# Linear attention and a token/channel mixer on one core: the last 64 rows of k and v on all 128 partitions, their product in quarters of the array, and two first attention tiles moved next to a last one

## The chip, the cores and the metric

The kernel runs on 1 core of one Trainium2 chip. The metric is the device time of one execution in microseconds. A core has five engines that run side by side and wait for each other by semaphores: TensorE (PE, matrix products, with its weight loads shown as PEld), VectorE (DVE), ScalarE (ACT), GpSimd (POOL) and SyncE (SP). All of them work on SBUF, a memory of 128 partitions. TensorE writes its sums to PSUM, 8 banks of 2 KB per partition, from which ACT and DVE copy them away. Transfers between HBM and SBUF are issued from a queue (here nearly all from SP's, the stores of the attention stage from POOL's) and are carried by 16 DMA engines.

## The reference

All arrays are float32; the batch is 8, 8 heads, 576 rows (seq), 64 columns per head.

```python
def _attn_ref(q, k, v, g_norm):
    kv = np.einsum('bhsd,bhse->bhde', k, v)
    out = np.einsum('bhsd,bhde->bhse', q, kv)
    rms = np.sqrt(np.mean(out * out, axis=-1, keepdims=True) + 1e-06)
    return (out / rms * g_norm).astype(np.float32)

def _moe_ref(x, w_tok1, w_tok2, w_ch1, w_ch2):
    xt = x.transpose(0, 2, 1)
    h = np.maximum(xt @ w_tok1, 0.0) @ w_tok2
    u = x + h.transpose(0, 2, 1)
    h2 = np.maximum(u @ w_ch1, 0.0) @ w_ch2
    return (u + h2).astype(np.float32)
```

The attention's output, laid out as (8, 576, 512), is x of the second part. w_tok1 is 576x256, w_tok2 256x576, w_ch1 512x1536, w_ch2 1536x512. The change concerns the first line alone, kv = k by v: for each batch and head a 64x64 matrix, summed over the 576 rows.

## The kernel before

**Stages.** Eight batches are worked in four pairs (numbered 0 to 3). For each pair come k by v (`kv`), attention (q by kv, `attend`), the normalisation, and token mixing (`tok1`, `tok2`). The channel mixing (w_ch1, w_ch2) of all batches follows from about 183 us to the end; it is a long run of full-array matmuls built on Strassen-like sums. While attention runs, the weights w_ch1 and w_ch2 are fetched and decoded from raw words on ACT and DVE (the "rounding" steps).

**Names.** `side` is 0 or 1, the batch within a pair. `half` is 0 or 1, the left or right 256 of the 512 columns (four heads). A pair has 9 tiles of 128 rows: groups c = 0 and 1 are side 0's four, c = 2 and 3 side 1's four, and c = 4 is one tile with the 64 remaining rows of both sides. J = 4, JJ = 5, HF = 64, LO = 512, DH = 256, D = 64.

**k and v in SBUF.** A side's k lies in `k_in[side]`, 128 partitions by 5 blocks (JJ) of 512 columns: four blocks with 512 rows, and block J with the last 64 rows on partitions 0 to 63. Partitions 64 to 127 of block J are filled with zeros once, for each side, by `zero_rows` (steps `zz0`, `zz1`, on POOL). `load` (steps `l0`, `l1`) issues, for k and then for v, one transfer of the 512 rows (`load_rows`) and two of 32 rows and 512 columns for the rest (`load_rem`). Six such loads are issued for pairs 1 to 3; pair 0 is loaded in another way and takes no part in the change except that its `zz` steps go.

**k by v.** `kv(side, half)` runs 20 matmuls: for two column groups i, five blocks j and two heads h, one matmul of 128 rows, 64 weights columns and 64 moving columns. Head h writes to PSUM partitions 64h to 64h + 63, so two matmuls use the two column halves of the array. Each (side, half) has its own bank, from a pool of two named "kv". `evict` (`e00`, `e01`, ...) copies a bank to `kvp[side]` on ACT.

**Attention.** `attend(c)` (step `a{c}`) runs 32 matmuls of 64x64 in the four quarters of the array: 64 rows (one head's part of kvp), 64 weights columns (half a tile of q). It takes two banks, from the pool "kv" for c = 0 and "o" otherwise. Steps `q`, `g`, `t` read these banks (square on ACT, times g on DVE, sum on DVE); `m`, `r`, `i` make the inverse root; `s`, `p`, `d` scale a tile on ACT, POOL or DVE. `a4` (`attend_rem`, tile name ps_r) is the tile of remaining rows, 16 matmuls of the same kind.

**Token mixing.** `h{side}{t}` (tok1) runs full-array matmuls (128x128 weights, 512 moving columns) over four tiles; `hr` adds the remaining rows, in two row halves. `u{i}` (tok2) makes tile i; `u8`, the tile of remaining rows, uses two column halves. Its result is added on DVE and stored by three transfers from POOL's queue.

**Order.** The order on every engine is the order of the strings that `play` reads: `start` (pair 0), `middle` (attention of pair 1 among the mixing of pair 0), two lists `steady` (pairs 2 and 3), then `last`. A leading "-" means a step of the pair before, a number means that many rounding steps. Each engine runs its part of this order strictly in turn. The first lines of `steady[0]` are:

```python
"kv00 kv01 e00 e01 -d40 f3", "-u8 -a3 -q30 -g31 -q31 -g30 -t30 -t31 -m3 -r3 -lq1",
"h00 -i3 -d31 -s30 l0 b00 1 1", "h01 f4 x01 1", "a0 q00 g01 q01 g00", "h10 t00 t01 b01 x10 1",
```

So side 0's k by v is followed by u8 and a3 of the pair before, then by h00 and h01; a0 stands between h01 and h10; `l0` loads the next pair's k and v for side 0; `f` steps fetch raw weights, `lq` and `lr` fetch q. Side 1's k by v (`kv10 kv11`) stands behind a1. In the trace all matmuls carry the helper's line 136, all transfers line 124 and ACT's copies line 133, so the tile names tell them apart: ps_kv is k by v, ps_o and ps_r attention, ps_h tok1, ps_u tok2.

## Time and profile before

| what | value |
|---|---|
| median of 3 runs | 770.01 us (770.0 to 770.4) |
| the profiled execution's own time | 769.76 us |
| its span, first to last instruction | 767.9 us |
| mean granted TensorE clock | 1.000 |
| ps_kv matmuls (all pairs) | 640 records, 20.9 us |
| ps_o matmuls in quarters | 768 records, 13.9 us |
| POOL memsets of k_in and v_in | 4, 0.52 us each |

A matmul of float32 leaves two records in the trace, so 640 records are 320 matmuls. Starts and durations are in microseconds from the start of the span. Matmuls overlap, so the time of a group is best read from its start to the next group's start; the recorded end of a group lies a little after that.

### The profile page before, as it was taken

Reading aid. Unit: us, or ns where it says so; the run is one execution under the profiler, and the core shown is the slowest. Engines: PE = TensorE matmul, PEld = TensorE weight load, DVE = VectorE, ACT = ScalarE, POOL = GpSimd, SP = SyncE. Lnnn points to the kernel's source line nnn. Section 1 sums busy time; section 2 is a strip of 40 time slices with the busy share of each in tenths; the row PEclk is TensorE's granted clock in tenths of the full one; section 3 lists DMA queues with packets and bytes.
Section 4 is the critical chain, followed back from the end, with each engine's and each line's share of the span. In section 5 each row is a group of like instructions: output and inputs, shape, how many; then the busy total and the mean of one; then the engine's idle time right before and its main releaser. Section 6 shows DMA issues by size and latency. Waiting matters only on the chain.

```text
span 767.9 us, 12737 instructions
## 1 busy us (share of the span) xinstructions
PE 761.9 (99%) x4694; PEld 615.4 (80%) x4694; DVE 644.9 (84%) x958; ACT 279.5 (36%) x563; POOL 112.8 (15%) x125
## 2 busy tenths in 40 slices
PE   9999999999999999999999999999999999999997
PEld 8655555446888888888888888888888888888887
DVE  4868886997757779899968989997898997798996
ACT  3656666773210332512234241123352223325221
POOL 1003030204410000002240002042000227000204
PEclk9999999999999999999999999999999999999999
DMA  9999997599699785589997578999659889755679
GB/s 356 379 366 382 353 376 281 178 326 340 244 290 318 291 284 167 172 271 217 221 230 251 154 226 213 261 185 265 195 154 295 159 227 211 199 150 158 156 188 120
DMA packets 137981, 188.28 MB, mean 245 GB/s; under 512 B 48704, under 2 KB 95808, under 8 KB 135872
## 3 DMA queue, kind: packets, MB, share of 16 engines
q1 hardware_dynamic: 102240, 168.72, 68.3%
q0 software_dynamic: 34848, 18.36, 15.9%
q8 instruction: 38, 0.62, 0.3%
q10 hardware_dynamic: 832, 0.39, 0.2%
q14 instruction: 23, 0.19, 0.1%
HBM read 138.28 MB, written 49.15 MB: 244 GB/s over the span
## 4 chain that ended last, share of the span: by engine, by line
PE 96%; DMA 2%; DVE 1%; SPq 0%; ACT 0%; issue 0%; DVEq 0%
PE ps_d L136 28%; PE ps_b L136 19%; PE ps_a L136 19%; PE ps_u L136 8%; PE ps_h L136 8%; PE ps_v L136 5%; PE ps_c L136 3%; PE ps_w L136 2%; PE ps_kv L136 2%; PE ps_o L136 2%; DMA raw<-in_moe_w_tok_dram 1%; DMA v_in<-in_k_dram 1%; PE ps_r L136 0%; DVE x L494 0%; DVE ms L522 0%; DVE w_tok L211 0%
## 5 line engine op out<-in xcount | busy, mean ns | idle before, releaser
L136 PE MATMUL ps_d<-ui,w 128*128 128x256 f32 x504 | 118.6, 379 | 0.0
L136 PEld LDWEIGHTS ps_d<-ui,w 128*128 128x128 f32 x504 | 96.0, 190 | 12.8
L133 ACT COPY ps_d<-ps_a 128x768 f32<-128x768 f32 (+1 forms) x56 | 32.0, 572 | 199.9 <-PE ps_a L136 196.9
L127 DVE TENSOR_TENSOR v<-v,v 128x1536 f32<-128x1536 f32 (+2 forms) x70 | 103.3, 1483 | 0.3
L136 PE MATMUL ps_b<-sv,w 128*128 128x256 f32 x324 | 78.9, 380 | 0.0
L136 PE MATMUL ps_a<-v,w 128*128 128x256 f32 x324 | 78.8, 379 | 0.0
L1275 POOL DMA_DIRECT2D out_dram<-us x24 | 26.8, 1835 | 291.8 <-ACT p L133 286.5
L136 PEld LDWEIGHTS ps_b<-sv,w 128*128 128x128 f32 x324 | 61.3, 190 | 8.8 <-issue 0.6
L136 PEld LDWEIGHTS ps_a<-v,w 128*128 128x128 f32 x324 | 61.7, 190 | 8.2
L136 PE MATMUL ps_u<-h,w_tok 128*128 128x512 f32 (+1 forms) x160 | 64.7, 599 | 0.0
L136 PE MATMUL ps_d<-v,w 128*128 128x256 f32 x258 | 62.7, 379 | 0.0
L130 ACT ACTIVATE v<-v 128x768 f32<-128x768 f32 (+1 forms) x54 | 42.6, 822 | 55.1 <-DVE v L127 52.3
L136 PE MATMUL ps_h<-x,w_tok 128*128 128x512 f32 x128 | 57.6, 601 | 0.7 <-DVE w_tok L211 0.6
L1275 POOL DMA_DIRECT2D out_dram<-r x40 | 41.3, 1926 | 102.0 <-ACT p L133 80.3
L136 PE MATMUL ps_d<-sv,w 128*128 128x256 f32 x228 | 55.4, 379 | 0.0
L136 PEld LDWEIGHTS ps_d<-v,w 128*128 128x128 f32 x258 | 49.1, 190 | 6.5
L136 PEld LDWEIGHTS ps_u<-h,w_tok 128*128 128x128 f32 (+1 forms) x160 | 25.7, 179 | 31.1 <-issue 26.7
L136 PEld LDWEIGHTS ps_d<-sv,w 128*128 128x128 f32 x228 | 43.4, 190 | 5.8
L136 PE MATMUL ps_a<-uT,w 128*128 128x256 f32 x192 | 46.7, 379 | 0.0
L136 PEld LDWEIGHTS ps_h<-x,w_tok 128*128 128x128 f32 x128 | 23.5, 190 | 28.3 <-issue 24.3
L136 PE MATMUL ps_b<-ui,w 128*128 128x256 f32 x168 | 40.9, 379 | 0.0
L136 PEld LDWEIGHTS ps_a<-uT,w 128*128 128x128 f32 x192 | 36.5, 190 | 4.9
(178 smaller groups left out, 1299.1 us busy)
## 6 DMA issues: line engine op xcount, KB each, us to landing
w<-parts SPq DMA_DIRECT2D x168, 384.0 KB
w<-parts SPq DMA_DIRECT2D x56, 192.0 KB
uT<-blocks SPq DMA_DIRECT2D x36, 256.0 KB
k_in<-in_k_dram SPq DMA_DIRECT2D x8, 1024.0 KB
v_in<-in_v_dram SPq DMA_DIRECT2D x8, 1024.0 KB
qT<-in_q_dram SPq DMA_DIRECT2D x8, 1024.0 KB
out_dram<-x POOLq DMA_DIRECT2D x16, 512.0 KB, 7.2
raw<-in_moe_w_ch_dram SPq DMA_DIRECT2D x8, 768.0 KB
```

Source lines behind the costliest of these rows:

```text
L127: keep(engine.tensor_tensor(out=o, in0=a, in1=b, op=op))
L130: keep(nc.scalar.activation(o, a, AF.Relu))
L133: keep(nc.scalar.copy(o, a))
L136: keep(nc.tensor.matmul(*a, **kw))
L1275: keep(nc.gpsimd.dma_start(to, t()[ds(b * Q, Q), at].rearrange("p n l j -> p n (l j)"), accum_op=ALU.add))
```

## The change

For pairs 1 to 3, the last 64 rows of k and v are laid on all 128 partitions: the left 256 columns on partitions 0 to 63, the right 256 on partitions 64 to 127, both in the first 256 columns of block J. `load_rem` issues four transfers of 32 rows and 256 columns per tensor instead of two of 32 rows and 512 columns. No zeros are needed, and `zero_rows` goes.

`kv` runs over four blocks (32 matmuls per side instead of 40). The remaining rows' part is a new function `kv_rem`, 8 matmuls per side of 64 rows, 64 weights columns and 64 moving columns, in the four quarters of the array; partition half a writes to the bank of column half a. It either opens the sums (step `kf`, before `kv`) or closes them (step `kr`, after it). Side 1 uses `kf1`, behind a1. Side 0 uses `kr0`: in `middle` right behind kv01, in `steady` behind u8, which is moved ahead of the two copies e00 and e01. In `middle`, e00 moves from behind kv00 to behind `kr0`. In both `steady` lists a0 moves from behind h01 to right behind the last pair's a3; the steps that read its banks stay where they were.

```diff
-        for n in range(0, HF, Q):
-            dma(dst[n:n + Q, J], t[b, LO + n:LO + n + Q].rearrange("(r e) d -> e r d", e=8))
+        for a in range(2):
+            for n in range(0, HF, Q):
+                dma(dst[ds(a * HF + n, Q), J, :DH],
+                    t[b, ds(LO + n, Q), ts(a, DH)].rearrange("(r e) d -> e r d", e=8))
...
-                o = kv_ps[side, half] = ps["kv"].tile([P, 2, P], F32, name="ps_kv", tag="kv")
+                o = kv_bank(side, half)
...
-                               start=(j == 0 and not (split and i)), stop=(j == JJ - 1), skip_group_check=True)
+                               start=(j == 0 and not (split and i if whole else seeded[side] or i)),
+                               stop=(j == JJ - 1 if whole else seeded[side] and j == J - 1), skip_group_check=True)
+
+        seeded = {s: False for s in range(2)}
+
+        def kv_bank(side, half):
+            if (side, half) not in kv_ps:
+                kv_ps[side, half] = ps["kv"].tile([P, 2, P], F32, name="ps_kv", tag="kv")
+            return kv_ps[side, half]
+
+        def kv_rem(side, first):
+            seeded[side] = first
+            o = [kv_bank(side, a) for a in range(2)]
+            for i in range(2):
+                for h in range(2):
+                    for a in range(2):
+                        r, at = ds(a * HF, HF), ds(i * P + h * D, D)
+                        matmul(o[a][ds(h * D, D), i, :D], lhsT=k_in[side][r, J, at], rhs=v_in[side][r, J, at],
+                               start=first and not i, stop=not first, skip_group_check=True)
...
-                          f"kv{s}{h}": do(kv, s, h), f"e{s}{h}": do(evict, s, h),
+                          f"kv{s}{h}": do(kv, s, h, range(JJ if whole else J)), f"e{s}{h}": do(evict, s, h),
+            steps |= {f"kf{s}": do(kv_rem, s, True), f"kr{s}": do(kv_rem, s, False)}
...
-    def zero_rows(side):
-        for t in (k_in, v_in):
-            keep(nc.gpsimd.memset(t[side][HF:, J], 0.0))
...
     middle = [
-        "h100 h110 h101 h111 w31 w22 w23 w24", "kv00 e00 -lq1 w32 w33 w34",
-        "h102 h112 h103 h113 w41 w42 w43 w44", "kv01 e01", "hr l0 z2",
+        "h100 h110 h101 h111 w31 w22 w23 w24", "kv00 -lq1 w32 w33 w34",
+        "h102 h112 h103 h113 w41 w42 w43 w44", "kv01 kr0 e00 e01", "hr l0 z2",
...
-        "kv10 kv11 e10 e11 t10 t11 m0 r0 lq0", "u3 z6 i0 d00 s01 d11 f1", "u4 l1", "a2 q20 g21 q21 g20",
+        "kf1 kv10 kv11 e10 e11 t10 t11 m0 r0 lq0", "u3 z6 i0 d00 s01 d11 f1", "u4 l1", "a2 q20 g21 q21 g20",
...
     steady = [[
-        "kv00 kv01 e00 e01 -d40 f3", "-u8 -a3 -q30 -g31 -q31 -g30 -t30 -t31 -m3 -r3 -lq1",
-        "h00 -i3 -d31 -s30 l0 b00 1 1", "h01 f4 x01 1", "a0 q00 g01 q01 g00", "h10 t00 t01 b01 x10 1",
-        "h11 1 x11 1", "hr z2 f5 f6", "a1 q10 g11 q11 g10 lq0", "kv10 kv11 e10 e11 t10 t11 m0 r0", "u0 i0 1",
+        "kv00 kv01 -u8 kr0 e00 e01 -d40 f3", "-a3 a0 -q30 -g31 -q31 -g30 -t30 -t31 -m3 -r3 -lq1",
+        "h00 -i3 -d31 -s30 l0 b00 1 1", "h01 f4 x01 1", "q00 g01 q01 g00", "h10 t00 t01 b01 x10 1",
+        "h11 1 x11 1", "hr z2 f5 f6", "a1 q10 g11 q11 g10 lq0", "kf1 kv10 kv11 e10 e11 t10 t11 m0 r0", "u0 i0 1",
```

The second `steady` list is changed in the same places. The steps `zz0` and `zz1` are gone from `start`.

## The prediction

> **What bounds the kernel now.** I read the page first (busy shares, then the chain of work that ended last), then TensorE's timeline through the attention stages, then who waits for whom, then the busy times by stretch.

> ```profile
> PE 761.9 (99%) x4694; PEld 615.4 (80%) x4694; DVE 644.9 (84%) x958; ACT 279.5 (36%) x563; POOL 112.8 (15%) x125
> ...
> PE 96%; DMA 2%; DVE 1%; SPq 0%; ACT 0%; issue 0%; DVEq 0%
> ```

> TensorE works 761.9 of 767.9 us and is 96% of the chain. From 30 us on its timeline has no idle time, so a microsecond taken from its instructions is a microsecond of the span, unless it turns into a wait. The part that the change touches looks like this (start, duration; one matmul leaves two records, so x80 is 40 matmuls):

> ```profile
> 35.93 1.39 PE L136 MATMUL ps_kv<-v_in,k_in 128*64 128x64 f32 x40
> 37.25 3.70 PE L136 MATMUL ps_h<-x,w_tok 128*128 128x512 f32 x8
> ...
> 57.76 1.16 PE L136 MATMUL ps_o<-kvp,qT 64*64 64x64 f32 x64
> 58.74 0.65 PE L136 MATMUL ps_r<-kvp,qR 64*64 64x64 f32 x32
> 59.31 1.13 PE L136 MATMUL ps_u<-h,w_tok 128*128 128x512 f32 x2
> ```

> ```profile
> 64.66 2.55 PE L136 MATMUL ps_kv<-v_in,k_in 128*64 128x64 f32 x80
> 67.04 1.89 PE L136 MATMUL ps_u<-h,w_tok 128*64 128x512 f32 x8
> 68.86 1.16 PE L136 MATMUL ps_o<-kvp,qT 64*64 64x64 f32 x64
> 69.95 7.13 PE L136 MATMUL ps_h<-x,w_tok 128*128 128x512 f32 x16
> 77.02 1.16 PE L136 MATMUL ps_o<-kvp,qT 64*64 64x64 f32 x64
> 78.11 7.13 PE L136 MATMUL ps_h<-x,w_tok 128*128 128x512 f32 x16
> 85.17 1.99 PE L136 MATMUL ps_h<-x,w_tok1r 64*128 64x512 f32 x8
> 87.09 1.16 PE L136 MATMUL ps_o<-kvp,qT 64*64 64x64 f32 x64
> 88.18 2.55 PE L136 MATMUL ps_kv<-v_in,k_in 128*64 128x64 f32 x80
> 90.67 1.55 PE L136 MATMUL ps_u<-h,w_tok 128*128 128x512 f32 x3
> ```

> From start to start a visit costs a fixed part and a slope. k by v (two halves of the array): 20 matmuls 37.25 - 35.93 = 1.32, 40 matmuls 90.67 - 88.18 = 2.49; so 1.17/20 = 58 ns each and 0.16 fixed. Quarters: 32 matmuls 69.95 - 68.86 = 1.09, 48 (ps_o and ps_r together) 59.31 - 57.76 = 1.55; so 0.46/16 = 29 ns each and 0.17 fixed. Full array (ps_h): 16 records 7.07 (77.02 - 69.95), 8 records 3.63 (40.88 - 37.25, the next start); so 0.43 per record and 0.19 fixed.

> **The change part by part.** All on TensorE's path unless said.

> 1. Remainder in quarters. Per side and pair, 8 matmuls of 128 rows (half of them zeros) leave k by v: 8 x 58 = 0.464. Eight of 64 rows come in: 8 x 29 = 0.232. Six sides (three pairs): 6 x -0.232 = -1.39. The 29 ns is from attention's matmuls, which have the same shape and alternate row halves and banks in the same way. Bounds: no overlap beyond today's two at a time would be 58 ns, a gain of 0; nothing in the rows allows under 27 (32 matmuls in 1.09 less two fixed parts of about 0.1). I take 29. What they cost to enter: for side 1 `kf1` stands behind a1, already in quarters; for side 0 of the two steady plays `kr0` stands between u8 and a3, ahead of a visit in quarters; nothing added. In the middle play `kr0` stands between kv01 and hr, a visit of its own: +0.17 once.

> 2. a0 next to a3 (two plays). From the start of a3 to the start of hr is 85.17 - 68.86 = 16.31 now. After: 64 matmuls in quarters 0.17 + 64 x 0.029 = 2.03, 32 records of ps_h 0.19 + 32 x 0.43 = 13.95, together 15.98. So -0.33 each, -0.66 in two. It is one fixed part of quarters and one of the full array less. [...]

> 3. The new order around u8 in the steady plays. Both copies e00 and e01 (ACT) now wait for `kr0`, which stands behind u8's 1.82 us; and a0 needs both copies (its operand kvp and the two banks that it writes). Behind a0 on TensorE stands everything else, h00 first. Its cover is a3 alone: 32 x 29 = 0.93. The copies:

> ```profile
> 68.91 0.41 ACT L133 COPY kvp<-ps_kv 128x128 f32<-128x128 f32 x2
> ```

> Two copies take 0.41. ACT starts 0.04 to 0.05 after the recorded end of a matmul group (kv01 ends 42.27, its copy starts 42.31), which is some 0.07 after the next group's start; DVE's result at 27.59 lets TensorE start at 27.65, and I take 0.06 for ACT too. So a0 may start 0.12 + 0.41 + 0.06 = 0.59 after a3's start, with 0.34 to spare. That holds if ACT is free. In pair 2 it decodes weights until 69.0; kv of 32 matmuls, u8 and `kr0` end near 64.66 + 1.92 + 1.82 + 0.23 = 68.63, so the copies end at 69.4 and a3 at 69.56, or 69.3 with the gains of the pair before: 0 to 0.2 late. In pair 3 ACT idles 2.55 us there. I take 0; bounds 0 and 2 x 0.9 (one more decode step ahead of the copies). On ACT q30 stands behind the copies, but it needs a3, which comes after `kr0` anyway. DVE takes u8's addition ahead of d40: d40 is 0.69 later and is needed by hr, 13 us on. u8's three stores on POOL's queue come no later. In the middle play e00 moves from 40.13 to about 42.3, behind it the ReLUs that start at 43.36; hr's 1.92 us covers both copies.

> 4. Transfers. Twelve remainder loads become four transfers each instead of two: 24 more on SP's queue, of half the size. Issuing one takes 0.69 (the median here is one of the remainder's; behind it, for whom SP's queue waited, in total, times, longest):

> ```profile
> L124 SPq DMA_DIRECT2D v_in<-in_v_dram x18: 333/687/719, 24.1 to 95.8; - x18
> ```

> ```profile
> SPq L124 <- DMA k_in<-in_k_dram: 14.1, 7, 4.1
> ```

> That is 2.8 us of queue time per load. Eight transfers are in flight at most: each waits on the counter of the one eight before, which is what the 14.1 us are. Queued behind are the fetches of weights and q. Their margins, from the packets in the trace: w_tok2's raw words have landed at 34.74 and ACT takes them at 38.90 (4.2); v of the third batch 43.5 against k by v at 51.64 (8); the second block of w_ch 61.97 against ACT at 67.27 (5.3). SP itself idles from 46.7 to 51.8, most of it waiting for attention's matmuls. Cost 0; bounds 0 and rival C.

> 5. The four memsets on POOL (0.52 each) go; POOL's next work is at 50.2. Nothing.

> Sum: -1.39 + 0.17 - 0.66 = -1.88, from the profiled execution's 769.76 to 767.9. That execution lies 0.25 under the median of the runs (770.01), so against the median I say 768.1.

> **The rivals.**

> A. The copies are late at both a0. For: ACT ran them 1.9 us after kv ended in pair 2, behind decode steps. Against: the 0.34 to spare, and ACT's idle time in pair 3. With one 0.9 us step ahead of them in each, a0 waits 0.9 - 0.34 = 0.56 twice: 769.2. [...] No wait of TensorE on a copy is in this trace.

> B. The gain is lost after attention.

> ```profile
> 150.00:160.00 10.00, 10.00 (x27) 4.25 (x24) 9.51 (x19) 6.25 (x17) 2.41 (x4) 1.00 0.89 293
> 160.00:170.00 10.00, 10.00 (x28) 4.07 (x27) 9.81 (x8) 6.58 (x13) 0.00 (x0) 1.00 1.02 307
> 170.00:180.00 10.00, 10.00 (x25) 4.51 (x24) 9.81 (x16) 7.25 (x14) 2.20 (x3) 1.00 1.01 369
> ```

> In each row stand the stretch, its length and the busy times of PE, PEld, DVE, ACT and POOL. DVE is busy 9.5 to 9.8 of 10 us here, and 9.83 in the stretch before: if it can't start earlier, TensorE meets it and waits the whole 1.88: 769.8 in the profile's time, 770.0. Against: at 138.96 DVE had waited 0.79 for TensorE, so it moves along; and TensorE's first product behind that stretch (182.65) has its DVE sums by 176.3.

> C, slower. Transfers late. If each load shifts the queue by its 2.8 and nothing absorbs it, the second block of w_ch, behind three loads, is 8.4 late; its margin is 5.3, so ACT stands 3.1 us before the decode step of 67.27, the copies e00, e01 behind it end at 72.4 and a0, due at 69.5, waits 2.9: 768.1 + 2.9 = 771.0. It decides from a lateness of 5.3 there. Against: SP's 5.1 us of idle time at 46.7 take most of it.

> D. The change doesn't do what it says: the eight matmuls run two at a time, because they add to banks that other tiles hold. Then 1.39 is lost: 769.5. Against: same shape and bank pattern as attention, though that one starts its banks afresh.

> **How the numbers follow.** Forecast 0.57, A 0.13, B 0.10, C 0.11, D 0.07; 0.02 for more than counted. A measurement of this kernel tells about 0.2% (1.5 us) from no change: faster means under 768.5. That takes the forecast but a few hundredths, and the 0.02: 0.56. Slower means over 771.5: most of C ends short of it, with doubled lateness it passes: 0.09. Within: 0.35. The forecast's own range is 767.2 (full-array fixed part 0.24 instead of 0.19 and more) to 768.7 (both a0 0.3 late). The range of 8 in 10 takes in A, B, D and the nearer part of C: 767.0 to 770.9.

> **What would show it.** k by v as x64 records taking 32 x 58 ns, then x16 records in some 0.25; a3 and a0 as one group of 2.0 us, the start of a3 to hr 16.0. Any idle time of TensorE between a3 and a0, named ACT kvp, is A; a wait on DVE between 140 and 190 is B; ACT waiting for raw at 67 is C; x16 records taking 0.46 is D. A faster profile without these pieces would make the reasons wrong even if the time is right.

## The result, and the profile after

| | before | after |
|---|---|---|
| median of 6 runs | 770.0 us (769.9 to 770.4) | 774.13 us (773.14 to 775.88) |
| ratio, 95% interval | | 1.0055 (1.0044 to 1.0065) |
| the profiled execution's own time, its span | 769.76, 767.9 us | 773.95, 772.1 us |
| mean granted TensorE clock | 1.000 | 0.998 |

The changed kernel is slower by 0.55% where 0.25% faster was forecast. The page of after still shows a kernel bound by TensorE, with 1.5 us more of busy time; the parts of the page that answer to those of before:

```profile
PE 763.4 (99%) x4694; PEld 615.0 (80%) x4694; DVE 644.4 (83%) x958; ACT 279.8 (36%) x563; POOL 110.8 (14%) x121
...
PE 95%; DVE 2%; DMA 1%; issue 1%; ACT 0%; DVEq 0%
```

"issue" has gone from 0% to 1% of the chain, and it is the clue. Who waited for whom, TensorE's rows (total, times, longest):

```profile
PE ps_o L136 <- issue: 2.6, 1, 2.6
...
PE ps_o L136 <- ACT kvp L133: 1.0, 1, 1.0
```

Both waits are in attention's matmuls, both new. TensorE's timeline through pair 2 and pair 3 (start, duration; in brackets the idle time before the group and what ended it):

```profile
36.19 1.15 PE L136 MATMUL ps_kv<-v_in,k_in 128*64 128x64 f32 x32
...
64.85 2.08 PE L136 MATMUL ps_kv<-v_in,k_in 128*64 128x64 f32 x64
66.77 1.89 PE L136 MATMUL ps_u<-h,w_tok 128*64 128x512 f32 x8
68.59 0.46 PE L136 MATMUL ps_kv<-v_in,k_in 64*64 64x64 f32 x16
68.87 1.11 PE L136 MATMUL ps_o<-kvp,qT 64*64 64x64 f32 x64
70.97 1.31 PE L136 MATMUL ps_o<-kvp,qT 64*64 64x64 f32 x64 [0.99 <-ACT kvp L133]
72.22 14.00 PE L136 MATMUL ps_h<-x,w_tok 128*128 128x512 f32 x32
86.15 1.99 PE L136 MATMUL ps_h<-x,w_tok1r 64*128 64x512 f32 x8
88.07 1.16 PE L136 MATMUL ps_o<-kvp,qT 64*64 64x64 f32 x64
89.05 2.67 PE L136 MATMUL ps_kv<-v_in,k_in 64*64 64x64 f32 x80
91.65 0.70 PE L136 MATMUL ps_u<-h,w_tok 128*128 128x512 f32 x1
...
111.35 1.81 PE L136 MATMUL ps_o<-kvp,qT 64*64 64x64 f32 x111
115.75 0.50 PE L136 MATMUL ps_o<-kvp,qT 64*64 64x64 f32 x17 [2.59 <-issue]
116.18 15.70 PE L136 MATMUL ps_h<-x,w_tok 128*128 128x512 f32 x32
131.80 1.99 PE L136 MATMUL ps_h<-x,w_tok1r 64*128 64x512 f32 x8
```

In pair 2, a3 and a0 should be one group; a0 starts late, behind the copies. In pair 3 the group breaks off after 111 of its 128 records and goes on 2.59 us later, waiting for nothing that the profile names. Then the 32 records of ps_h take 131.80 - 116.18 = 15.62 instead of 86.15 - 72.22 = 13.93. The busy times by stretch say why (the number behind POOL's is the granted clock):

```profile
114.00:116.00 2.00, 0.25 (x16) 0.26 (x17) 1.84 (x4) 0.60 (x2) 0.63 (x2) 1.00 1.03 392
116.00:118.00 2.00, 2.00 (x20) 0.91 (x11) 1.71 (x6) 0.98 (x5) 0.00 (x0) 0.60 0.94 307
118.00:120.00 2.00, 2.00 (x4) 0.85 (x3) 2.00 (x6) 1.65 (x6) 0.00 (x0) 0.54 1.06 303
120.00:122.00 2.00, 2.00 (x6) 0.92 (x5) 2.00 (x7) 0.00 (x0) 0.00 (x0) 1.00 1.02 351
```

Behind the stall the clock was 0.60 and 0.54 for two stretches of 2 us: (0.40 + 0.46) x 2 = 1.72 us lost, which is the 1.69 of the longer ps_h group. The balance on TensorE, each term from start to start against before:

| place | change, us |
|---|---|
| start of pair 0, ahead of every changed matmul | +0.26 |
| middle: kv00, kv01 and kr0 (36.19 to 42.38, before 35.93 to 42.20, both with the ps_h between) | -0.08 |
| side 1: a1, kf1, kv10, kv11 (88.07 to 91.65 = 3.58, before 87.09 to 90.67 = 3.58), three times | 0.00 |
| side 0 steady: kv, u8, kr0 (64.85 to 68.87 = 4.02, before 4.20), twice | -0.36 |
| pair 2, start of a3 to hr: 17.28, before 16.31 | +0.97 |
| pair 3, the same: 20.45, before 16.31 | +4.14 |
| sum | +4.93 |

The first row need not be the change's: e2 below, whose program is before's up to pair 2, starts the same matmuls at 36.19 too, 0.26 later. TensorE's last matmul ends 4.94 later in the trace. The span is only 4.2 longer, since 0.74 less lies behind the last matmul. From 132 us on the distance to before stays at 4.94, so nothing was lost or won in the channel mixing.

### The profile page after: what moved, and what is told of

Same layout as the page of the kernel before. It is cut to its first block, busy times and chain, and to the rows that moved or that the text cites. A ratio compares the mean times of both kernels' runs of the same rounds, so it can differ in the third digit from the quotient of the medians.

```text
span 772.1 us, 12759 instructions
## 1 busy us (share of the span) xinstructions
PE 763.4 (99%) x4694; PEld 615.0 (80%) x4694; DVE 644.4 (83%) x958; ACT 279.8 (36%) x563; POOL 110.8 (14%) x121
## 4 chain that ended last, share of the span: by engine, by line
PE 95%; DVE 2%; DMA 1%; issue 1%; ACT 0%; DVEq 0%
PE ps_d L136 28%; PE ps_b L136 19%; PE ps_a L136 19%; PE ps_h L136 8%; PE ps_u L136 7%; PE ps_v L136 5%; PE ps_c L136 3%; PE ps_w L136 2%; PE ps_kv L136 2%; PE ps_o L136 2%; DMA raw<-in_moe_w_ch_dram 1%; PE ps_j L136 1%; PE ps_r L136 0%; DVE x L514 0%; DVE x L586 0%
## 5 line engine op out<-in xcount | busy, mean ns | idle before, releaser
L136 PE MATMUL ps_d<-ui,w 128*128 128x256 f32 x504 | 118.6, 379 | 0.0
L136 PEld LDWEIGHTS ps_d<-ui,w 128*128 128x128 f32 x504 | 95.8, 190 | 13.0
L133 ACT COPY ps_d<-ps_a 128x768 f32<-128x768 f32 (+1 forms) x56 | 32.0, 572 | 199.9 <-PE ps_a L136 196.9
L136 PE MATMUL ps_b<-sv,w 128*128 128x256 f32 x324 | 78.9, 379 | 0.0
L136 PE MATMUL ps_a<-v,w 128*128 128x256 f32 x324 | 78.7, 379 | 0.0
L136 PEld LDWEIGHTS ps_b<-sv,w 128*128 128x128 f32 x324 | 61.2, 190 | 8.9 <-issue 0.5
L136 PEld LDWEIGHTS ps_a<-v,w 128*128 128x128 f32 x324 | 61.6, 190 | 8.4
L136 PE MATMUL ps_u<-h,w_tok 128*128 128x512 f32 (+1 forms) x160 | 64.7, 599 | 0.0
L136 PE MATMUL ps_d<-v,w 128*128 128x256 f32 x258 | 62.7, 379 | 0.0
L136 PE MATMUL ps_h<-x,w_tok 128*128 128x512 f32 x128 | 58.8, 613 | 0.5 <-DVE w_tok L213 0.5
L136 PE MATMUL ps_d<-sv,w 128*128 128x256 f32 x228 | 55.4, 379 | 0.0
L136 PEld LDWEIGHTS ps_d<-v,w 128*128 128x128 f32 x258 | 48.9, 190 | 6.6
L136 PEld LDWEIGHTS ps_u<-h,w_tok 128*128 128x128 f32 (+1 forms) x160 | 25.6, 179 | 31.1 <-issue 26.7
L136 PEld LDWEIGHTS ps_h<-x,w_tok 128*128 128x128 f32 x128 | 24.2, 194 | 30.0 <-issue 26.0
L136 PEld LDWEIGHTS ps_d<-sv,w 128*128 128x128 f32 x228 | 43.3, 190 | 5.9
L136 PE MATMUL ps_a<-uT,w 128*128 128x256 f32 x192 | 46.7, 379 | 0.0
L136 PE MATMUL ps_b<-ui,w 128*128 128x256 f32 x168 | 40.8, 379 | 0.0
L136 PEld LDWEIGHTS ps_a<-uT,w 128*128 128x128 f32 x192 | 36.5, 190 | 5.0
```

Source lines behind the costliest of these rows:

```text
L133: keep(nc.scalar.copy(o, a))
L136: keep(nc.tensor.matmul(*a, **kw))
```

## The experiments

The theories, as numbered in the expectations. Theory 1: kr0, a3 and a0 in a row use up TensorE's instructions faster than they arrive, and the merged visit stalls. Theory 2: the doubled transfers make it late, through the raw words that ACT waits for. Theory 3: something else, fixed at that place, that the profile does not name. Theory 4, from e5 on: the eight matmuls of `kf1` lose their gain to the waits for eight small transfers.

What theory 1 rests on is in the page: queue q8 carries instructions in 38 packets, 0.62 MB, so 16 KB each. TensorE left 2 x 4694 records of matmuls and weight loads, with its waits and drains 9,697 instructions, about 38 x 256 = 9,728: by this estimate one block is 256 instructions. A float32 matmul takes four (two records of each kind). kr0, a3 and a0 are 72 matmuls, 288 instructions, in about 2.2 us; 16 records of ps_h are 32 instructions in 7 us. The DMA view of after for 113 to 114.5 us has exactly one such packet (packets, MB, share):

```profile
q8 instruction: 1, 0.02, 4.4%
```

In the trace it runs from 113.25 to 114.30, and TensorE, idle for 2.59 us, goes on at 115.75, 1.45 later.

**Merge undone (e1).** Everything of the change but a0's place, in both lists:

```diff
-"-a3 a0 -q30 ..."    ... "q00 g01 q01 g00"
+"-a3 -q30 ..."       ... "a0 q00 g01 q01 g00"
```

> The changed kernel with one part undone: a0 stands behind h01 again in both steady lists; the quarters, kr0 behind u8 and the 24 additional transfers stay. Theory 1 (TensorE's own instructions arrive too late when kr0, a3 and a0 stand together: 72 matmuls, four instructions each, used up in 2.2 us): kr0 and a3 alone are 160 instructions, so no idle time there, the clock stays at 1.00 from 110 to 120, and the time is 770.0 less 0.08 (middle) less 2 x 0.18 (kr0 in the steady lists) = 769.5, within 0.4. Theory 2 (the additional transfers alone, which made the second block of w_ch late): the wait of ACT for raw words at 67 stays and TensorE still loses 1 us or more: 771 or above.

Measured 769.08 us (768.5 to 770.14, 10 runs), ratio 0.9983 (0.9974 to 0.9992). ACT's timeline in pair 2:

```profile
70.69 0.90 ACT L183 ACTIVATE w_ch<-raw 128x768 f32<-128x768 f32 x1 [3.06 <-DMA raw<-in_moe_w_ch_dram]
...
72.30 0.40 ACT L133 COPY kvp<-ps_kv 128x128 f32<-128x128 f32 x2
```

ACT waits for raw words even longer than in after (3.06 against 1.49), and its copies come later, yet TensorE has no wait here, since a0 stands behind h00 and h01. Theory 2 by itself falls: of the two, late transfers cost TensorE time only where a0 follows a3 (0.99 us in after, none in e1). The time came out 0.42 under theory 1's 769.5. TensorE's last matmul ends 0.18 earlier than before's, which is what the terms of the balance without the merge give, 0.26 - 0.08 - 0.36. The rest of the gain of 1.2 by the medians lies behind the last matmul or in the scatter, and is not explained.

**Merge alone (e2).** Before, with a0 behind a3:

```diff
-"-u8 -a3 -q30 ..."   ... "a0 q00 g01 q01 g00"
+"-u8 -a3 a0 -q30 ..." ... "q00 g01 q01 g00"
```

> The kernel before with a0 moved behind a3 in both steady lists and nothing else: k by v in halves with 40 matmuls, zeros, two transfers per tensor, the copies ahead of u8. Theory 1 (instructions late): a3 and a0 together are 256 instructions in 1.9 us; in pair 3 TensorE stands idle 1 to 2.8 us inside a0 with no releaser named, and the granted clock falls behind it; time 770.0 - 0.7 + 1 to 2.8 + up to 1.7 = 770.5 to 773.8. Theory 2 (transfers): no idle time at a0, 769.3.

Measured 770.56 us (769.67 to 770.93, 10 runs), ratio 1.0003 (0.9994 to 1.0013). TensorE's timeline in both pairs:

```profile
69.12 2.10 PE L136 MATMUL ps_o<-kvp,qT 64*64 64x64 f32 x128
...
110.45 1.96 PE L136 MATMUL ps_o<-kvp,qT 64*64 64x64 f32 x115
112.56 0.45 PE L136 MATMUL ps_o<-kvp,qT 64*64 64x64 f32 x13 [0.15 <-issue]
```

In pair 2 the merge works: a3 to h00 in 2.02 us. In pair 3 the group breaks at nearly the same place, 115 records instead of 111, with none of the new transfers and no kr0. The time lies in theory 1's range, but the idle time is 0.15 and not 1 to 2.8, and the clock did not fall. The stall is small because the whole of u8, slow at 1.82 us, stands among the 256 instructions ahead of it: they lasted 3.7 us here, 2.4 in after, and the block, 110.18 to 111.14, had nearly come.

**Two transfers (e3).** After, with 64 rows and 256 columns per transfer:

```diff
-            for n in range(0, HF, Q):
-                dma(dst[ds(a * HF + n, Q), J, :DH],
-                    t[b, ds(LO + n, Q), ts(a, DH)].rearrange("(r e) d -> e r d", e=8))
+            dma(dst[ds(a * HF, HF), J, :DH],
+                t[b, LO:, ts(a, DH)].rearrange("(r e) d -> e r d", e=16))
```

> The changed kernel with two transfers per tensor for the remaining rows instead of four (64 rows of 256 columns each), so as many as before the change. Theory 2 (transfers alone): ACT no longer waits for raw words at 67, TensorE not at a0 of pair 2, and the time is the forecast's, 768.1 to 769. Theory 1 (instructions) with theory 2 for pair 2 only: ACT's wait and the 0.99 idle behind the copies go, but the idle time inside a0 of pair 3 stays (2 to 3 us, and the lower clock behind it), and pair 2, no longer held up by the copies, may run dry as well: 772 to 776.

Measured 770.19 us (768.34 to 770.86, 10 runs), ratio 0.9998 (0.9989 to 1.0007), between the two theories, and in neither's range. TensorE's timeline:

```profile
68.73 2.05 PE L136 MATMUL ps_o<-kvp,qT 64*64 64x64 f32 x128
...
87.64 2.45 PE L136 MATMUL ps_kv<-v_in,k_in 64*64 64x64 f32 x80
...
109.73 1.91 PE L136 MATMUL ps_o<-kvp,qT 64*64 64x64 f32 x115
112.94 0.45 PE L136 MATMUL ps_o<-kvp,qT 64*64 64x64 f32 x13 [1.31 <-issue]
```

Both theories hold a part. The raw words land at 62.7 instead of 68.6, ACT does not wait and pair 2 is whole, which is theory 2's part. The stall of pair 3 stays, at 115 records, but is 1.31 long, because the block came at 110.51 to 111.43. The four records more are eight instructions: ahead of the stall TensorE has 35 waits here and 43 in after, counted with its one drain. The clock stayed at 1.00 behind it. Side 1 now gains: a1 to u0 in 90.02 - 86.66 = 3.36 instead of 3.58.

**64 fewer instructions ahead (e4).** After, with 5 warm-up matmuls of 512 columns at the start instead of 21 of 128. This moves the edge of every later block (where one block ends and the next begins) by 64 instructions, 32 records, past the end of the merged visit, and leaves the work behind the start alone (the tile `ones` is widened to 512 columns):

```diff
-        "j21 zk00 ..."
+        "j5 zk00 ..."
...
-            matmul(late["junk"][:, :P], lhsT=ones, rhs=ones, start=True, stop=True)
+            w = DM if n == 5 else P
+            matmul(late["junk"][:, :w], lhsT=ones[:, :P], rhs=ones[:, :w], start=True, stop=True)
```

> The changed kernel with 64 TensorE instructions less ahead of everything: the 21 warm-up matmuls of 128 columns at the start are 5 of 512 columns, about as long. Nothing near a0 is touched. Theory 1: TensorE's instructions come in blocks of 256, and the block that was awaited inside a0 of pair 3 is now awaited 64 instructions later in the program, behind a0 and inside h00, where 64 instructions take many us; the idle time of 2.6 inside a0 goes or falls under 1, the clock stays up, and the time falls to 769.5 to 771. Theory 3 (a0 waits for data: copies, q or banks): the idle time stays where it is at 2 to 3 us, 774.

Measured 769.53 us (767.55 to 771.86, 10 runs), ratio 0.9989 (0.9977 to 1.0002). The profiled run is the shortest of the ten, and shows TensorE with no stall in either pair, although its block arrived as late as in after, at 113.69 to 114.76: TensorE needed it only at 117.98, inside h00. This speaks against theory 3, a stall fixed at that place; e8 settles it. The other nine runs left no trace; that their scatter of 4.3 us is the raw words' lateness is argued only.

**Two transfers, no merge (e5).** The edits of e3 and e1 together.

> The changed kernel with two transfers per tensor for the remaining rows (64 rows of 256 columns) and with a0 behind h01 again. Theory 1 (instructions late where kr0, a3 and a0 stand together) and theory 4 (the eight matmuls of kf1 lose their gain to the waits for eight small transfers): no idle time; side 1's a1 with kf1 and kv take 3.40 as with two transfers, not 3.58; the sum is 0.08 (middle) + 2 x 0.18 (kr0) + 3 x 0.18 (kf1) = 0.98 less than before: ratio 0.9987. If the waits did not cost, as with four transfers and a0 moved back: 0.9983 there, no difference from it.

Measured 768.93 us (768.65 to 769.07, 11 runs), ratio 0.9983 (0.9975 to 0.9992). No stall; TensorE's last matmul ends 0.89 earlier than before's. That is the remainder's work without the merge: 0.08 + 0.36 and some 0.2 at each side 1, less 0.27 at the start. Whether theory 4 holds the times can't tell: e5 and e1 have the same ratio, 0.9983, where it asked for a difference. The traces can: a1 to u0 in pair 2 takes 90.23 - 86.84 = 3.39 here and 3.61 in e1, and TensorE's last matmul ends 0.71 earlier than e1's.

**Two transfers, merge, fewer ahead (e6).** The edits of e3 and e4 together.

> The changed kernel with two transfers per tensor and with 64 TensorE instructions less at the start (5 warm-up matmuls of 512 columns instead of 21 of 128), a0 next to a3 as in the change. Theory 1: the block of instructions is awaited inside h00, no idle time at a0, and both gains are there: 0.98 + 0.66 = 1.6 less than before, ratio 0.9979. Rival: the idle time comes back at another place of the visits in quarters; ratio 0.999 or more.

Measured 767.66 us (767.48 to 768.07, 6 runs), ratio 0.9967 (0.9955 to 0.9979). TensorE's timeline in pair 3:

```profile
109.32 0.46 PE L136 MATMUL ps_kv<-v_in,k_in 64*64 64x64 f32 x16
109.61 2.05 PE L136 MATMUL ps_o<-kvp,qT 64*64 64x64 f32 x128
111.58 14.00 PE L136 MATMUL ps_h<-x,w_tok 128*128 128x512 f32 x32
125.51 1.99 PE L136 MATMUL ps_h<-x,w_tok1r 64*128 64x512 f32 x8
```

This is the visit as the prediction drew it: 1.97 us for a3 and a0, and 125.51 - 109.61 = 15.90 to hr (predicted 15.98). The kernel is faster than before and after.

**The control (e7).** Before, with e4's edit alone.

> A control: the kernel before with the 5 wide warm-up matmuls instead of 21, nothing else. Theory 1: nothing near a0 to save, the start is as long; ratio 0.9995 to 1.0005. If the wide warm-up is itself worth something (a faster start), 0.999 or less, and what the other kernels gained with it has to be read less that.

Measured 769.65 us (769.42 to 769.73, 10 runs), ratio 0.9991 (0.9982 to 1.0). So the other warm-up is worth some 0.4 us (the interval runs from nothing to 1.4). Over this control e6 gains 769.65 - 767.66 = 2.0 us by the medians. In the profiled executions it is 769.42 - 767.77 = 1.65, and TensorE's last matmul ends 1.64 earlier.

**32 fewer instructions ahead (e8).** After, with 13 warm-up matmuls of 208 columns. If the count of instructions sets the place, the stall must move by 16 records, from 111 to 127.

```diff
-        "j21 zk00 ..."
+        "j13 zk00 ..."
...
+            w = 208 if n == 13 else P
```

> The changed kernel with 32 TensorE instructions less ahead (13 warm-up matmuls of 208 columns instead of 21 of 128). Theory 1 says where the idle time stands: 32 instructions are 16 matmul records, so in pair 3 it stands 16 records later than in the changed kernel, where it came after 111 records of a3 and a0 with 17 left: after 127, with 1 left, still 1.5 to 2.5 us long. Theory 3 (data): it stays after 111.

Measured 770.93 us (770.6 to 774.24, 6 runs), ratio 1.0016 (1.0004 to 1.0028). The profiled run is the longest of the six; four of the others lie at 770.6 to 771.2 and left no trace. Its TensorE timeline:

```profile
72.15 1.54 PE L136 MATMUL ps_o<-kvp,qT 64*64 64x64 f32 x64 [2.19 <-ACT kvp L133]
...
114.17 2.04 PE L136 MATMUL ps_o<-kvp,qT 64*64 64x64 f32 x127
118.23 0.27 PE L136 MATMUL ps_o<-kvp,qT 64*64 64x64 f32 x1 [2.03 <-issue]
```

The stall stands after 127 records, to the record, and theory 3 falls. Pair 2 lost 2.19 to late raw words again.

The count can be made in full. TensorE's matmul records, weight loads and waits (its one drain counted among them) from the start of the trace to the stall are 3,009 in each of the four runs that stalled: 2 x 1,483 records and 43 waits in after and e8, 2 x 1,487 and 35 in e2 and e3. The stalls of pair 3 side by side (the block's packet, and the start of the instruction behind those 3,009, from the traces):

| kernel | records before the stall | block's packet | instruction 3,010 starts | idle |
|---|---|---|---|---|
| after | 111 | 113.25 to 114.30 | 115.75 | 2.59 |
| e2 | 115 | 110.18 to 111.14 | 112.56 | 0.15 |
| e3 | 115 | 110.51 to 111.43 | 112.94 | 1.31 |
| e8 | 127 | 115.83 to 116.87 | 118.23 | 2.03 |
| e4 | all 128 | 113.69 to 114.76 | 117.98 | none |
| e6 | all 128 | 113.67 to 114.69 | 119.41 | none |
| before | a3 and a0 apart | 111.10 to 112.06 | 119.23 | none |

In every stalled run TensorE goes on 1.36 to 1.51 us after the end of the packet. The packet ended 2.0 to 3.8 us after TensorE had passed the edge before, 256 instructions earlier; these 256 lasted 1.9 to 3.7 us in the stalled runs and 10.7 in before, where the ps_h between a3 and a0 are among them. What sets the 2.0 to 3.8 was not tested. Pair 2 is whole because its edges stand elsewhere: after 1,729 instructions early in a3 (68.94 in after, the block had landed at 65.56), and after 1,985 inside h00 or later.

**Four transfers in before (e9).** Twice the transfers in the old layout, 16 rows of 512 columns each:

```diff
-        for n in range(0, HF, Q):
-            dma(dst[n:n + Q, J], t[b, LO + n:LO + n + Q].rearrange("(r e) d -> e r d", e=8))
+        for n in range(0, HF, 16):
+            dma(dst[n:n + 16, J], t[b, LO + n:LO + n + 16].rearrange("(r e) d -> e r d", e=8))
```

> The kernel before with four transfers per tensor for the remaining rows instead of two (16 rows of 512 columns each), nothing else. Theory 2 (the number of transfers delays what is queued behind them, since only eight are in flight): the second block of w_ch, whose packets ended at 61.97 before and at 66.5 to 69.8 in the four kernels with four transfers, ends there here too, and ACT waits 1 to 3 us for it at 67. In the old order a0 stands 8 us behind the copies, so TensorE doesn't wait: 769.8 to 770.6. Rival: the lateness came from the new layout (1 KB pieces, 128 partitions): the block ends near 62, no wait of ACT.

Measured 769.8 us (769.41 to 771.42, 10 runs), ratio 1.0 (0.999 to 1.0009). ACT's timeline in pair 2:

```profile
69.59 0.94 ACT L181 ACTIVATE w_ch<-raw 128x768 f32<-128x768 f32 x1 [2.02 <-DMA raw<-in_moe_w_ch_dram]
...
71.23 0.42 ACT L133 COPY kvp<-ps_kv 128x128 f32<-128x128 f32 x2
```

The number of transfers makes the raw words late (69.1; 61.97 in before), with the old layout and the same bytes. The 66.5 to 69.8 of the expectation are starts of the last packet; by the ends, as the 61.97, they are 66.7 to 70.0. TensorE, without the merge, does not notice.

## Why the prediction was wrong

TensorE's last matmul was forecast 1.88 earlier and came 4.93 later by the balance. Of the 6.81 between, 4.47 are pair 3's visit (step 2), 1.30 pair 2's (step 4), 0.78 the remainder (step 1) and 0.26 the start.

**1. Remainder in quarters: right at side 0, mis-sized at side 1.** Forecast were -1.22 in all, measured -0.44. The middle's side 0, predicted at -0.232 + 0.17 = -0.06, measured -0.08. kr0 in the steady plays gave -0.18 each for -0.232: 68.59 to 68.87 is 0.28, not 0.23. The missing 0.05 comes back in a3 behind it, which takes 69.97 - 68.93 = 1.04 in e1 for 1.09 before; so kr0 pays the entry into quarters and a3 does not, as step 1 had it:

```profile
68.93 1.11 PE L136 MATMUL ps_o<-kvp,qT 64*64 64x64 f32 x64
69.97 5.42 PE L136 MATMUL ps_h<-x,w_tok 128*128 128x512 f32 x12
```

kf1 is the term that was mis-sized: the gain of each side 1 is 0.00, so its eight matmuls cost about as much as the eight that they replace, 0.464 instead of 0.232. It is not rival D, two at a time: the same matmuls took 0.28 as kr0, and with half the transfers (e3, e5, e6) side 1 gains 0.18 to 0.22. In the trace of after gaps of 0.06 and 0.14 us lie behind kf1's first two records. The first matmuls of kf1 open the sums and so carry the waits for the eight remainder transfers, and waits for several counters are instructions of their own on TensorE (306 in after, 297 in before and e3); at this place after has four of them, of two counters each, at 88.80 to 89.14. The prediction counted the matmuls that come in and not the waits that they carry.

**2. a0 next to a3: the step that failed.** "-0.33 each" is right in size where instructions are there: a3 to hr takes 15.95 in e2's pair 2 and 15.90 in both pairs of e6 (0.05 of that is kr0's), against 16.31. Both fixed parts show in e2's pair 2: a3 and a0 together take 71.14 - 69.12 = 2.02, where each visit alone took 1.09, and the ps_h behind them 85.07 - 71.14 = 13.93, where the two groups took 7.07 and 7.06. In the trace of before k by v, too, takes less ahead of u8, which has its form (128*64), than ahead of the full array: 67.04 - 64.66 = 2.38 for 90.67 - 88.18 = 2.49. But the prediction priced the matmuls by their duration only and put the supply of their instructions at nothing. Before, a visit in quarters used 128 instructions in 1.09 us and the ps_h behind it 32 in 7 us: the block that TensorE needed at 119.23 had landed at 112.06. kr0, a3 and a0 in a row use 288 in 2.2 us, and in pair 3, where a block's edge falls late in a0, TensorE of after stood idle from 113.16 and the block landed at 114.30. The visit took 116.18 - 111.35 = 4.83 in pair 3 where e6 takes 1.97, +2.86, and the clock behind it +1.69. No rival had it, though the page of before has q8's row too.

**3. The copies on ACT: right under its condition.** In pair 3 and in every whole pair 2 the 0.34 to spare was enough. "That holds if ACT is free" failed in pair 2 by step 4. Rival A's form (a0 waiting for kvp) appeared once, for rival C's reason.

**4. Transfers, "Cost 0": wrong.** Rival C had the place and the chain. The second block of w_ch landed at 68.6, 6.6 later than 61.97, past the margin of 5.3; ACT waited 1.49, the copies ran at 70.66, a0 waited 0.99:

```profile
69.05 0.95 ACT L183 ACTIVATE w_ch<-raw 128x768 f32<-128x768 f32 x1 [1.49 <-DMA raw<-in_moe_w_ch_dram]
69.87 0.90 ACT L188 ACTIVATE raw<-raw 128x768 uint32<-128x768 uint32 x1
70.66 0.42 ACT L133 COPY kvp<-ps_kv 128x128 f32<-128x128 f32 x2
```

What failed is the argument against C, that SP's idle 5.1 us would take most of the lateness. The second block is the second of two fetches. SP's queue issued it in before at 52.28:

```profile
52.28 0.79 SPq L124 DMA_DIRECT2D raw<-in_moe_w_ch_dram x1
```

and in after at 57.50, behind more and slower issues:

```profile
49.06 6.37 SPq L124 DMA_DIRECT2D v_in<-in_v_dram x5
55.54 0.39 SPq L124 DMA_DIRECT2D raw<-in_moe_w_ch_dram x1
...
57.50 0.46 SPq L124 DMA_DIRECT2D raw<-in_moe_w_ch_dram x1
```

Five issues stretch over 6.37 us, where the three of before took 1.90: the extra transfers wait for counters of transfers still in flight (from 40 to 76 us SP's queue waited 17.0 us for transfers in after, 10.9 in before), and the time in which SP was idle is used up by them. As for size, C gave 2.9. The idle time was 0.99, and from the start of a3 to hr pair 2 lost 17.28 - 15.90 = 1.38 against e6.

**5. Sum and rivals.** B did not happen: the distance to before does not change between 132 us and the end. The sum of the forecast, -1.88 on TensorE, is nearly what e6, which has half the transfers, shows against its control, -1.64. e6 starts 0.24 later than the control, which no run explains; the rest adds up to about -1.9, with the parts near their forecasts. The range ended at 770.9 because it held only lateness of the kinds that the trace of before shows; the visit that ran out of instructions was outside it.

## What to carry to other kernels

Before putting small matmuls next to each other, count their instructions as well as their time: here 288 in 2.2 us outran a supply of 38 packets for 9,697 instructions, some 256 at a time. An edge moved by 64 instructions made the difference between e3's 770.2 and e6's 767.7 us; the control explains 0.4 of it, and the stalled visit of e3's trace, 3.60 us for e6's 1.97, another 1.6. A merge also takes away the cover of whatever the second visit waits for: the same late raw words cost TensorE nothing in e1 and e9, and 0.99 to 2.19 us in after and e8. On a queue whose transfers wait for earlier ones, as SP's does here, count the transfers and not only their bytes: in e9 twice the remainder transfers, with the same bytes, brought the raw words at 69.1 instead of 61.97.

## What the runs showed of the hardware

```profile
72.00:74.00 2.00, 1.85 (x65) 1.73 (x66) 2.00 (x5) 0.77 (x3) 0.97 (x2) 0.77 1.05 383
74.00:76.00 2.00, 2.00 (x3) 0.79 (x3) 1.89 (x4) 0.64 (x2) 0.71 (x2) 0.50 1.00 383
76.00:78.00 2.00, 2.00 (x5) 0.85 (x4) 1.66 (x6) 0.97 (x5) 0.00 (x0) 0.87 0.93 307
```
